# A decode kernel whose loads leave from two queues: every second half of K and V, behind the first ones, is issued from ScalarE's queue, and the order of all work is searched anew

## The chip, the cores and the metric

The kernel runs on one core of a Trainium2 chip. The core has five engines, each with an in-order stream of instructions of its own: TensorE (PE in the profile) for matrix products, VectorE (DVE), ScalarE (ACT), GpSimd (POOL) and SyncE (SP). Sixteen DMA engines move data between HBM and the on-chip memory SBUF; an engine that issues a transfer (here SP, and after the change also ACT) only hands it over, and the transfer then waits in a queue that belongs to the issuing engine. The engines meet through semaphores: an instruction waits until a counter has reached a value.

The metric is device time in microseconds of the whole program. A quoted trace row gives start, duration, engine, source line (L1214 is line 1214 of the kernel), operation and number of instructions.

## What is computed

Two decoder layers, run twice with the same weights, on four tokens (one new position of each of four sequences): attention over a window of a K/V cache, then a gated feed-forward block (FFN). The part that sets the time is the attention:

```python
B, Sq, D = 4, 1, 448
Hq, Hkv, Sk, Dh = 16, 8, 8192, 256
W = min(4096, max(256, Sk // 4))            # 2048 positions
q = (x @ wq).reshape(B, Sq, Hq, Dh).transpose(0, 2, 1, 3)
k = jnp.repeat(k_cache[:, :, Sk - W:, :], rep, axis=1)
v = jnp.repeat(v_cache[:, :, Sk - W:, :], rep, axis=1)
scores = jnp.einsum("bhqd,bhkd->bhqk", q, k) * (Dh ** -0.5)
o = jnp.einsum("bhqk,bhkd->bhqd", _softmax(scores), v)
return o.transpose(0, 2, 1, 3).reshape(B, Sq, Hq * Dh) @ wo
...
x = x + _A_ref(_layernorm(x), A_k_cache, A_v_cache, A_wq, A_wo)
x = x + _B_ref(_layernorm(x), B_w_gate, B_w_up, B_w_down)
x = x + _A_ref(_layernorm(x), A_k_cache, A_v_cache, A_wq, A_wo)
x = x + _B_ref(_layernorm(x), B_w_gate, B_w_up, B_w_down)
```

Each kv head of each token has a K and a V of 2048 x 256 bf16 values, 1 MB each. Both layers read the same cache, and a token's second layer needs the result of its first one, so either its K and V are kept on chip between the two uses or they are loaded twice.

## The kernel before

**Halves and slots.** K and V of a kv head are loaded in halves of 512 KB. In this text K103.1 is half 1 of K of token 1, layer 0, kv head 3 (the program's own order: token, layer, head). A half lies in one of 31 slots of the buffer `kv`; seven more slots (31 to 37) hold the query weights `wq` until the last query projection has read them. The table `SLOTS` gives each load its slot, written here as K103.1@14. A load may be issued only when the last reader of what lay in its slot is done. That reader is the `scores` operation for a half of K (L982) and one `pv` operation for a half of V (L1057). Of the eight heads of a token the last six of its first layer are kept (`KEEP_K`, `KEEP_V`): 6 heads x 4 halves = 24 slots stay occupied until that token's second layer has used them.

**Groups.** Two kv heads of one token make a group. On its way a half of K is turned on VectorE (`tr`, L948). Then follow `scores` (PE, L982), the maximum (DVE, L995), `spread` (PE, L1000), its negative (DVE, L1009), the exponential (ACT, L1013), `turn` (PE, L1026), a copy `pT` (ACT, L1035), `total` (PE, L1043), four `pv` (PE, L1057), a copy `oh` (ACT, L1072), its second step (DVE, L1074), `flip` (PE, L1080) and the scaled result `oT` (DVE, L1090); then the output projection (PE, L1102 and L1110). There are 32 groups, in the order of the table `PLAN`; for every token four of layer 0 and four of layer 1. Of its four layer-1 groups three use the kept heads and load nothing, and the one with heads 0 and 1 loads again.

**Between the layers of a token** stands a serial piece: the rows of the output projection are folded into the residual (L857 on ACT, L859 on DVE, L867 on PE), then the norm (L599 on PE), the FFN (`gu`, 112 matmuls of L785; a tanh on ACT, L805; `down`, 56 matmuls of L826, which needs the weights `wd`), a norm again, the query projection (L671 on PE, L677 on ACT, L687, L701) and the spread queries `qc` (DVE, L706) and `qe` (POOL, L987). Only then can the layer-1 `scores` of that token start and give back the kept slots of K, and the `pv` behind them those of V. This piece, from the landing of the token's last kept half to its first layer-1 `scores`, is called the handover here; there are four, one for each token.

**What sets the order.** Nothing is decided while the program is built. The tables `SEQ_PE`, `SEQ_DVE`, `SEQ_ACT`, `SEQ_POOL` and `SEQ_SP` list, by number, every operation of each engine in the order of its stream (a number counts calls of `g.op` and `g.dma`). They come from a search done ahead. `schedule` (L235) reads them, gives the loads their slots, adds the waits that a reused slot needs, and drops waits that others imply. In `SEQ_SP` a pair "124+126" is one transfer of a whole K into two neighbouring slots. All loads are issued by SP, in order: a load whose slot is not free yet holds up all behind it.

**Fillers.** A "w" in `SEQ_PE` is a matmul that adds zero to the bank `Ab` (L1214). It has no result; it keeps PE occupied. `HELD` says how many fillers each DVE or ACT operation on that bank has to wait for.

Of the kernel before, what the change touches and what calls it, by code (L numbers as in the profile page):

```python
# [38 lines left out]
SLEAD = -3.4  # L39
# [43 lines left out]
).split()  # L83
SEQ_DVE = (
# [18 lines left out]
).split()  # L103
SEQ_ACT = (
# [5 lines left out]
).split()  # L110
SEQ_POOL = (
# [8 lines left out]
).split()  # L120
SEQ_SP = (
# [7 lines left out]
).split()  # L129
# [1161 lines left out]
```

## Time and profile before

| | |
|---|---|
| time, median of 3 runs | 283.76 us (281.19 to 288.03) |
| span of the profiled execution, first to last instruction | 283.0 us |
| busy: PE / DVE / POOL / ACT | 210.4 / 168.6 / 77.2 / 50.9 us |
| moved by the DMA engines | 96.67 MB, mean 342 GB/s |
| issued by SP: halves of V, halves of K, whole K | 80, 66, 7 |
| fillers (L1214) | 147, 51.0 us busy |
| mean clock granted to TensorE | 0.895 |

The profiled execution has no total of its own beside the span; the median of the runs is 0.8 us above it. "Busy" counts an engine's instructions, not its waits, and PE's busy time is modelled at its end, so it doesn't say that PE is at its limit. The DMA engines' rate over time says more here: it is flat near 408 GB/s for long stretches and lower in others.

### The profile page before, as it was taken

What the parts mean: (1) busy time and instruction counts of PE and PEld (TensorE: products, weight loads), DVE (VectorE), ACT (ScalarE), POOL (GpSimd) and SP (SyncE); (2) the same over time, 40 slices, a digit from 0 to 9 for tenths busy, and PEclk for the clock granted to TensorE, in tenths of its full rate; (3) what the DMA queues carried; (4) which work ended last, traced back from release to release, by engine and by line L of the source; (5) the groups of instructions that cost most, each with busy time, mean ns of one, the idle gap of its engine ahead of it and who ended that gap; (6) DMA issues with size and microseconds to landing.
All of it is one profiled execution on the core that took longest, in us unless ns stands there. A gap on an engine that the chain in (4) does not pass through costs nothing.

```text
span 283.0 us, 9526 instructions
## 1 busy us (share of the span) xinstructions
PE 210.4 (74%) x4204; PEld 120.8 (43%) x4204; DVE 168.6 (60%) x511; ACT 50.9 (18%) x123; POOL 77.2 (27%) x202
## 2 busy tenths in 40 slices
PE   0757557586778886789887876798685787888986
PEld 0322124233644543347453432375453346554672
DVE  8745374158226795573755858656756378548831
ACT  0030002011102412112121212112130221034311
POOL 1352103001303432013253241123341221341650
PEclk9997757779789999799997979999795999999995
DMA  6999999999999999968799999948799997899300
GB/s 258 424 414 401 413 410 402 407 401 406 377 390 408 400 408 406 409 278 307 290 324 403 411 406 408 397 170 295 254 316 412 415 405 266 286 341 415 125 2 3
DMA packets 27752, 96.67 MB, mean 342 GB/s; under 512 B 2747, under 2 KB 6847, under 8 KB 26431
## 3 DMA queue, kind: packets, MB, share of 16 engines
q1 hardware_dynamic: 27703, 96.06, 88.0%
q8 instruction: 33, 0.54, 0.8%
q14 instruction: 8, 0.07, 0.1%
q10 hardware_dynamic: 8, 0.00, 0.0%
HBM read 96.05 MB, written 0.00 MB: 339 GB/s over the span
## 4 chain that ended last, share of the span: by engine, by line
DMA 30%; PE 27%; SPq 23%; DVE 12%; issue 3%; ACT 3%; POOL 0%
DMA half<-in_A_k_cache_dram 13%; DMA half<-in_A_v_cache_dram 11%; SPq L555 10%; DVE half L948 8%; SPq L958 8%; DMA wd_sb<-in_B_w_down_dram 6%; PE A L1214 5%; PE Y L1057 5%; PE S L982 4%; PE Z L785 3%; SPq L944 3%; SPq L942 3%; PE Z L826 2%; PE A L1110 2%; DVE oh L1074 1%
## 5 line engine op out<-in xcount | busy, mean ns | idle before, releaser
L948 DVE STREAM_TRANSPOSE half<-half 128x1024 uint32<-128x1024 uint32 x80 | 98.0, 1233 | 16.3 <-DMA half<-in_A_k_cache_dram 15.9
L1214 PE MATMUL A<-identb,small 128*128 128x512 bf16 x147 | 51.0, 452 | 7.4 <-DVE A L478 5.5
L1070 POOL TENSOR_TENSOR small<-small 128x4 f32<-128x4 f32 x32 | 32.4, 1015 | 68.0 <-DVE small L1048 61.7
L982 PE MATMUL S<-half,qe 128*8 128x256 bf16 (+1 forms) x1040 | 40.8, 305 | 12.0 <-DVE half L948 11.1
L1057 PE MATMUL Y<-half,pT 128*8 128x256 bf16 x1024 | 42.2, 296 | 7.3 <-DMA half<-in_A_v_cache_dram 3.9
L982 PEld LDWEIGHTS S<-half,qe 128*8 128x8 bf16 x1040 | 25.4, 92 | 26.1 <-DVE half L948 15.5
L987 POOL TENSOR_TENSOR qe<-qc,tiny 128x64 bf16<-128x64 bf16 x64 | 17.2, 292 | 60.1 <-PE S L982 46.4
L1013 ACT ACTIVATE praw<-S,small 104x256 bf16<-104x256 f32 x32 | 15.1, 473 | 81.7 <-DVE small L1009 81.2
L1057 PEld LDWEIGHTS Y<-half,pT 128*8 128x8 bf16 x1024 | 22.2, 90 | 17.8 <-DMA half<-in_A_v_cache_dram 5.3
L995 DVE TENSOR_REDUCE tiny<-S 104x1 bf16<-104x256 f32 x32 | 13.3, 418 | 19.0 <-PE S L982 19.0
L1072 ACT ACTIVATE oh<-Y 128x256 bf16<-128x256 f32 x32 | 12.3, 383 | 66.3 <-PE Y L1057 61.9
L1214 PEld LDWEIGHTS A<-identb,small 128*128 128x128 bf16 x147 | 13.0, 109 | 20.4 <-issue 7.4
L1074 DVE SCALAR_TENSOR_TENSOR oh<-oh,small,Y 128x256 bf16<-128x256 bf16 x32 | 15.0, 468 | 11.0 <-ACT oh L1072 10.4
L1110 PE MATMUL A<-wo_sb,oT 128*4 128x448 bf16 x220 | 17.2, 380 | 0.8 <-DVE oT L1090 0.6
L1080 PE MATMUL Y<-tiny,oh 128*128 128x4 bf16 x64 | 6.6, 172 | 15.1 <-DVE oh L1074 15.0
L1048 DVE TENSOR_REDUCE small<-Y 128x4 f32<-128x64 f32 x32 | 7.0, 218 | 13.8 <-PE Y L1043 12.1
L1026 PE MATMUL Y<-selt,praw 104*64 104x48 bf16 x256 | 10.1, 197 | 5.9 <-ACT praw L1013 5.5
L1080 PEld LDWEIGHTS Y<-tiny,oh 128*128 128x128 bf16 x64 | 4.2, 103 | 22.5 <-DVE oh L1074 19.6
L1035 ACT ACTIVATE pT<-Y 128x192 bf16<-128x192 f32 x32 | 10.5, 329 | 15.6 <-PE Y L1026 15.3
L1026 PEld LDWEIGHTS Y<-selt,praw 104*64 104x64 bf16 x256 | 6.7, 113 | 12.6 <-ACT praw L1013 9.9
L671 PE MATMUL Z<-half,xn 128*5 128x512 bf16 x160 | 10.2, 379 | 2.2 <-DVE st L606 0.8
L612 POOL TENSOR_SCALAR st<-st 128x1 f32<-128x1 f32 x16 | 4.4, 274 | 26.4 <-DVE st L606 26.4
(125 smaller groups left out, 219.7 us busy)
## 6 DMA issues: line engine op xcount, KB each, us to landing
half<-in_A_v_cache_dram SPq DMA_DIRECT2D x80, 512.0 KB, 12.1
half<-in_A_k_cache_dram SPq DMA_DIRECT2D x66, 512.0 KB, 10.3
half<-in_A_k_cache_dram SPq DMA_DIRECT2D x7, 1024.0 KB, 17.2
wo_sb<-in_A_wo_dram SPq DMA_DIRECT2D x8, 448.0 KB, 16.8
half<-in_A_wq_dram SPq DMA_DIRECT2D x3, 1024.0 KB, 9.0
wd_sb<-in_B_w_down_dram SPq DMA_DIRECT2D x1, 1568.0 KB, 17.1
wg_sb<-in_B_w_gate_dram SPq DMA_DIRECT2D x1, 1344.0 KB, 17.3
wu_sb<-in_B_w_up_dram SPq DMA_DIRECT2D x1, 1344.0 KB, 16.6
```

What stands on the lines that cost most here:

```text
L555: g.dma(rank, nbytes, lambda e: e.dma_start(dst, src), f"w{nw[0]}", w=key if isinstance(key, tuple) else (key,), run=run)
L948: return e.transpose(a, a)
L958: g.dma(pp + VLAG, 1 << 19, lambda e, cell=cell, hv=hv, vsrc=vsrc: e.dma_start(unit(cell), vsrc[hv]), None, w=(f"v{t}_{kvh}_{hv}",), run=4 ...
L982: last = e.matmul(Sb[s_][qd:qd + 8, c0:c0 + rhs.free_size()], lhsT=qe[q_][:, P, ce, :, :].rearrange("p a n -> p (a n)"), rhs=rhs, start=(c ...
L987: g.op(POOL, 0.25, pos - SLEAD - 1, lambda e, P=P, t=t, kvh=kvh: e.tensor_tensor(qe[q_][:, P, :, :, :], qc[t][:, kvh, :, :].unsqueeze(2).b ...
L1013: return e.activation(praw[0:R, 0:128 * n].rearrange("p (g r l) -> p g r l", g=2 * n, l=2), Sb[s_][0:R, 0:128 * n].rearrange("p (l g r) -> ...
L1026: last = e.matmul(Yb[p_][64 * h:64 * h + 64, c0:c0 + (48 if n == 2 else 32)], lhsT=praw[0:R, 64 * gg:64 * gg + 64], rhs=w, start=(gg == 0) ...
L1057: last = e.matmul(Yb[p_][32 * gg:32 * gg + M, 256:512], lhsT=pT[pt][:, gg, 2 * a + hv, 4 * P:4 * P + M] if n == 2 else p1[:, gg % 2, 2 * a ...
L1070: g.op(POOL, 0.69, pos, lambda e: e.tensor_tensor(ri[p_][:, 0:2 * n], rs[p_][:, 0:2 * n], expo[:, 1:1 + 2 * n], op=ALU.pow), r=(f"rs{p_}", ...
L1074: g.op(DVE, 0.43, pos, lambda e: e.scalar_tensor_tensor(out=oh[:, :], in0=oh[:, :], scalar=lomask[:, 0:1], in1=Yb[p_][:, 256:512], op0=ALU ...
L1110: last = e.matmul(Ab[32 * k:32 * k + B, 0:D], lhsT=oT[oi][:, k % 2, k // 2, :], rhs=wo_sb[:, 4 * kvh + k, :], start=False, stop=False, ski ...
L1214: return e.matmul(Ab[:, 0:512], lhsT=zero[:, 0:1].broadcast_to([128, 128]), rhs=identb[:, :].unsqueeze(1).broadcast_to([128, 4, 128]), sta ...
```

## The change

The order of the groups is the same, and so are the slots' number, the heads kept, the bytes moved and what every operation computes. What differs:

1. **Two issuing queues.** 64 of the 153 transfers of K and V, all behind the first ones, carry an "a" in `SEQ_SP`. `schedule` moves them to ScalarE: the transfer stands at its place in `SEQ_ACT`, among the exponentials and copies, with its wait for the slot.
2. **Steps.** `PLAN` had 28 steps, four of them with two groups; it has 32 of one group each. A step ends with its output projection. The form of a group with one head and its constants (`sel1`, `far1`, seven small DVE operations at the start) are taken out; no group had that form. A "/" in `PLAN` would split `scores` in two operations; no group uses it.
3. **All tables are new**: the five orders, `SLOTS`, `HELD`. `SEQ_PE` has 31 fillers, not 147. `SLOTS` leaves no pair of K halves over 15 slots apart (before, K111 was, which took 16 matmuls more).

What the numbers in the tables stand for, in the places that matter (A: is ACT's queue):

```
first loads, before: X WQ2 K000 WQ1 V001.0 WQ3 WQ0 K001.1 K001.0 V000.1 K003 WO0 V000.0 WO5 K004 ...
first loads, after:  K103.0@0 X K004 K005 K100.0@5 K007 K002 K101.0@10 K001.0 K006 K101.1@14 K001.1 WQ3 WQ2 WQ1 WQ0
                     K100.1@16 K003 V000.1 K000 V002.1 WO1 V001.1@23 V003.1 V004.1 WO0 V001.0@26 V002.0 V000.0 WO4 V004.0
                     WO5 A:V005.0 wgb WO2 WO7 WO3 wub V003.0 V007.1 V006.1 A:V007.0 A:V005.1 V006.0 wga WO6 V100.0@26
                     wua wd A:V100.1@23 V101.0@5 K103.1@14 A:V101.1@10 A:K105.1@16 K102.0@26 A:K104.1@23 K107.0@5
                     A:K104.0@10 K105.0@8 A:K102.1@17 ...
handover of token 1, from its last kept half:
  before: V106.0 | K200.0 K201.0 K201.1 V201.0 V200.1 V200.0 V201.1 K010.0 K010.1 K011.1 K011.0 V010.0 V010.1
          V011.1 K203.1 K203.0 V011.0 V203.0 | K205.0
  after:  A:V107.0 | A:K011.0 K011.1 A:V200.0 V200.1 A:V201.0 V201.1 V011.0 A:V010.0 V010.1 A:K202.1 A:V011.1 K203.0
          A:K207.1 K205.0 K204.1 A:K203.1 A:K202.0 | K205.1
handover of token 2:
  before: V206.0 | K301.0 K300.0 K301.1 V300.1 V301.0 V301.1 V300.0 K304.1 K305.1 K302.0 K304.0 K303.1 K303.0
          K302.1 | V306.1
  after:  V207.1 | A:K306.1 V300.0 A:K302.1 V301.0 V301.1 A:K306.0 A:K302.0 V300.1 A:K303.1 K305.1 A:K305.0 | K304.1
handover of token 3:
  before: V307.1 | K111.0 K110.1 K110.0 K210.0 V110.1 K210.1 V110.0 V111.0 K211.0 K211.1 V211.1 V111.1 V210.0 | V210.1
  after:  A:V307.1 | K111.1 A:V111.1 V110.1 A:K210.1 V110.0 A:V111.0 K211.0 A:K210.0 K211.1 A:V210.1 K310.1
          A:K310.0 | V210.0
ACT, after, token 0: ... d.rowsA d.tanh A:K104.1 d.q0 d.q1 oh A:K104.0 A:K102.1 A:K106.0 A:V105.1 exp pT A:K201.1 A:V105.0 exp ...
```

The first bar stands behind the token's last kept half, the second ahead of the first load whose slot waits for that token's layer 1 (for token 3: for its query projection).

The core of the diff, with the long tables cut:

```diff
@@ schedule @@
         seq = {PE: SEQ_PE, DVE: SEQ_DVE, SCA: SEQ_ACT, POOL: SEQ_POOL, SP: SEQ_SP}
-        pairs = [[self.ops[int(y)] for y in x.split("+")] for x in SEQ_SP if "+" in x]
-        order = {e: [self.ops[int(y)] for x in s if x[0] not in "wq" for y in x.split("+")] for e, s in seq.items()}
+        pairs = [[self.ops[int(y)] for y in x.strip("a").split("+")] for x in SEQ_SP if "+" in x]
+        order = {e: [self.ops[int(y)] for x in s if x[0] not in "wq" for y in x.strip("a").split("+")] for e, s in seq.items()}
+        loads = [o for o in order[SP] if o.cell is not None]
+        for x in SEQ_SP:
+            if x[0] == "a":
+                for y in x.strip("a").split("+"):
+                    self.ops[int(y)].eng = SCA
+        order[SP] = [o for o in order[SP] if o.eng == SP]
         assert sum(map(len, order.values())) == len(self.ops) == len({o for s in order.values() for o in s})
-        loads = [o for o in order[SP] if o.cell is not None]
...
-        order[SP] = [o for o in order[SP] if o not in second]
+        for e in (SP, SCA):
+            order[e] = [o for o in order[e] if o not in second]
@@ group @@
-            def scores(e):
+            def scores(e, Ps):
                 last = None
-                X, J = 4 // n, 2 * n
                 for ce in range(8):
-                    for x in range(X):
-                        for P in range(n):
+                    for x in range(2):
+                        for P in Ps:
...
-            o = g.op(PE, (0.87, 1.72)[n - 1], pos - SLEAD, scores, ...
+            for Ps in ([(P,) for P in range(len(members))] if apart[gi] else [tuple(range(len(members)))]):
+                kw = dict(acc=(f"s{s_}",)) if Ps[0] else dict(w=(f"s{s_}",))
+                o = g.op(PE, (0.86, 1.72)[len(Ps) - 1], pos - SLEAD, lambda e, Ps=Ps: scores(e, Ps), ...
...
@@ tables @@
 PLAN = (
-    "000+001", "002+003 004+005", "006+007", "100+101", "012+013", ...
-    "212+213 214+215", "216+217 302+303", "306+305", "304+307", "110+111", "210+211 316+313", "314+315",
+    "000+001", "002+003", "004+005", "006+007", "100+101", "012+013", ...
+    "212+213", "214+215", "216+217", "302+303", "306+305", "304+307", "110+111", "210+211", "316+313", "314+315",
...
+    "128 165 196 150 127 158 121 224 195 225 a201 111 187 262 188 113 164 239 233 a238 a202 232 110 261 322 112 114 "
+    "a323 328 434 a329 a469 426 a463 502 a461 467 a428 582 a496 504 a472 498 588 584 a590 a471 a621 430 a431 465 a436 "
...
 HELD = (
-    "0 44 48 57 72 76 86 96 96 100 100 109 112 122 131 131 133 133 138 138 139 139 139 139 139 139 139 139 141 141"
+    "0 4 4 4 8 8 8 10 10 12 12 12 12 15 29 29 29 29 30 30 30 30 30 30 30 30 30 30 30 30"
```

More of the change, by code (lines that the diff above doesn't have):

```diff
@@ L357, in plan @@
 def plan():
-    return [() if st == "F" else tuple(tuple((int(c[0]), int(c[1]), int(c[2])) for c in b.split("+")) for b in st.split()) for st in PLAN]
+    return [() if st == "F" else tuple(tuple((int(c[0]), int(c[1]), int(c[2])) for c in b.replace("/", "+").split("+")) for b in st.split()) for st in PLAN]
 def build(nc, A_x, A_k_cache, A_v_cache, A_wq, A_wo, B_x, B_w_gate, B_w_up, B_w_down, out):
@@ L401, in build @@
         selt = [at(f"selt{h}", [128, 4, 12], BF16) for h in range(2)]
-        sel1 = [sb(f"sel1{h}", [128, 4, 2, 2, 2], BF16) for h in range(2)]
         small = sb("small", [128, 17 + 2 * NS + 8 * NY + 2 * B], FP32)
@@ L408, in build @@
         fars = small[:, 11:14].bitcast(BF16)
-        far, far1 = fars[:, 0:4].rearrange("p (P o n) -> p P o n", P=2, o=1), fars[:, 4:6].rearrange("p (o n) -> p o n", o=1)
+        far = fars[:, 0:4].rearrange("p (P o n) -> p P o n", P=2, o=1)
         nmask = rs[0]
@@ L436, in build @@
         rest = plan()
+        apart = ["/" in b for st in PLAN for b in st.split()]
         ends = {t: max(i for i, s in enumerate(rest) for b in s for h in b if h[:2] == (t, 1)) for t in range(B)}
@@ L513, in build @@
                 op0=ALU.add, op1=ALU.mult), r=("rs0", "negm0"), w=("far",))
-        for n_ in range(2):
-            g.op(DVE, 0.1, R0, lambda e, n_=n_: e.tensor_tensor(
-                negm[1][:, n_:n_ + 1], nmask[:, n_:n_ + 1], nmask[:, 2 + n_:3 + n_], op=ALU.add), r=("rs0",), w=("negm1",))
-        g.op(DVE, 0.1, R0, lambda e: e.tensor_scalar(
-            far1[:, 0, :], negm[1][:, 0:2], negm[0][:, 1:2], FAR, op0=ALU.add,
-            op1=ALU.mult), r=("negm0", "negm1"), w=("far1",))
-        for h in range(2):
-            for y in range(2):
-                g.op(DVE, 0.16, R0, lambda e, h=h, y=y: e.tensor_copy(sel1[h][:, :, :, y, :], ivq[:, :, h:4:2, :]),
-                     r=("identb",), w=(f"sel1{h}{y}",))
         for s_ in range(NS):
@@ L930, in group @@
             p_, s_, q_ = gi % NY, gi % NS, gi % NQ
-            pt, pos, n = gi % NP, members[-1][0], len(members)
-            R, N, lag = (104, 256, 0.0) if n == 2 else (104, 128, 0.0)
+            pt, pos, n, R, N = gi % NP, members[-1][0], 2, 104, 256
             kcs, kks, vss, free_k, free_v = [], [], [], [], []
@@ L972, in group @@
             g.tag = ("g",) + members[-1][1:]
-            def scores(e):
+            def scores(e, Ps):
                 last = None
-                X, J = 4 // n, 2 * n
                 for ce in range(8):
-                    for x in range(X):
-                        for P in range(n):
+                    for x in range(2):
+                        for P in Ps:
                             qd = 64 * P + 32 * x
-                            for i, (c0, rhs) in enumerate(keys(kcs[P], J * x, J, ce)):
+                            for i, (c0, rhs) in enumerate(keys(kcs[P], 4 * x, 4, ce)):
                                 last = e.matmul(Sb[s_][qd:qd + 8, c0:c0 + rhs.free_size()],
@@ L990, in group @@
                     r=(f"qc{t}_{kvh}",) + tuple(f"qmask{a}" for a in range(4)), w=(f"qe{q_}_{P}",))
-            o = g.op(PE, (0.87, 1.72)[n - 1], pos - SLEAD, scores, r=tuple(k for kk in kks for k in kk) + tuple(f"qe{q_}_{P}" for P in range(n)),
-                     w=(f"s{s_}",), bank=(f"S{s_}",))
-            o.rel = tuple(c for kc, fr in zip(kcs, free_k) if fr for c in kc)
-            o.pairs = tuple(kcs)
+            for Ps in ([(P,) for P in range(len(members))] if apart[gi] else [tuple(range(len(members)))]):
+                kw = dict(acc=(f"s{s_}",)) if Ps[0] else dict(w=(f"s{s_}",))
+                o = g.op(PE, (0.86, 1.72)[len(Ps) - 1], pos - SLEAD, lambda e, Ps=Ps: scores(e, Ps),
+                         r=tuple(k for P in Ps for k in kks[P]) + tuple(f"qe{q_}_{P}" for P in Ps), bank=(f"S{s_}",), **kw)
+                o.rel = tuple(c for P in Ps if free_k[P] for c in kcs[P])
+                o.pairs = tuple(kcs[P] for P in Ps)
             g.op(DVE, (0.23, 0.36)[n - 1], pos, lambda e: e.tensor_reduce(
@@ L1000, in spread @@
                 e.matmul(Sb[s_][0:R, 256:288], lhsT=identb[0:R, 0:R],
-                         rhs=far[0:R, :, :, :].broadcast_to([R, 2, 8, 2]) if n == 2 else
-                         far1[0:R, :, :].broadcast_to([R, 16, 2]), start=True, stop=False, skip_group_check=True)
+                         rhs=far[0:R, :, :, :].broadcast_to([R, 2, 8, 2]), start=True, stop=False, skip_group_check=True)
                 return e.matmul(
@@ L1007, in spread @@
                     skip_group_check=True)
-            g.op(PE, 0.18, pos, spread, r=(f"pmax{s_}", "identb", "far", "far1"), w=(f"m{s_}",), bank=(f"S{s_}",))
+            g.op(PE, 0.18, pos, spread, r=(f"pmax{s_}", "identb", "far"), w=(f"m{s_}",), bank=(f"S{s_}",))
             g.op(DVE, 0.13, pos, lambda e: e.tensor_reduce(
@@ L1021, in turn @@
                     for h in range(2):
-                        if n == 2:
-                            c0, w = 48 * gg, selt[h][0:R, :, :].rearrange("p a u -> p (a u)")
-                        else:
-                            c0, w = 32 * gg, sel1[h][0:R, :, :, :, :].rearrange("p x a y n -> p (x a y n)")
-                        last = e.matmul(Yb[p_][64 * h:64 * h + 64, c0:c0 + (48 if n == 2 else 32)],
-                                        lhsT=praw[0:R, 64 * gg:64 * gg + 64], rhs=w,
+                        last = e.matmul(Yb[p_][64 * h:64 * h + 64, 48 * gg:48 * gg + 48],
+                                        lhsT=praw[0:R, 64 * gg:64 * gg + 64],
+                                        rhs=selt[h][0:R, :, :].rearrange("p a u -> p (a u)"),
                                         start=(gg == 0), stop=False, skip_group_check=True)
                 return last
-            g.op(PE, (0.12, 0.22)[n - 1], pos, turn, r=("praw", "selt0", "selt1") +
-                 tuple(f"sel1{h}{y}" for h in range(2) for y in range(2)), w=(f"yp{p_}",), bank=(f"Y{p_}",))
-            PW = 192 if n == 2 else 64
-            pf = pT[pt][:, :, :, :].rearrange("p g a u -> p (g a u)")[:, 0:PW]
-            p1 = pf[:, 0:64].rearrange("p (c x a y n) -> p c x a y n", c=2, x=4, a=2, y=2)
-            g.op(SCA, (0.2, 0.27)[n - 1], pos, lambda e: e.activation(pf, Yb[p_][:, 0:PW], ACT.Copy),
+            g.op(PE, (0.12, 0.22)[n - 1], pos, turn, r=("praw", "selt0", "selt1"), w=(f"yp{p_}",), bank=(f"Y{p_}",))
+            pf = pT[pt][:, :, :, :].rearrange("p g a u -> p (g a u)")
+            g.op(SCA, (0.2, 0.27)[n - 1], pos, lambda e: e.activation(pf, Yb[p_][:, 0:192], ACT.Copy),
                 r=(f"yp{p_}",), w=(f"pT{pt}",), bank=(f"Y{p_}",))
@@ L1042, in total @@
                 for P in range(n):
-                    last = e.matmul(sums[:, :, P, :], lhsT=onesb[:, 0:1].broadcast_to([128, 128]), rhs=pw[:, :, 8 * P:8 * P + 2] if n == 2 else
-                                    p1[:, :, :, :, 0, :].rearrange("p c x a n -> p (c x a) n"),
+                    last = e.matmul(sums[:, :, P, :], lhsT=onesb[:, 0:1].broadcast_to([128, 128]), rhs=pw[:, :, 8 * P:8 * P + 2],
                                     start=False, stop=False, skip_group_check=True)
@@ L1053, in pv @@
                 last = None
-                M = 4 if n == 1 else 8
                 for a in range(2):
                     for gg in range(4):
-                        last = e.matmul(Yb[p_][32 * gg:32 * gg + M, 256:512],
-                                        lhsT=pT[pt][:, gg, 2 * a + hv, 4 * P:4 * P + M] if n == 2 else
-                                        p1[:, gg % 2, 2 * a + gg // 2, hv, :, :].rearrange("p y n -> p (y n)"),
+                        last = e.matmul(Yb[p_][32 * gg:32 * gg + 8, 256:512],
+                                        lhsT=pT[pt][:, gg, 2 * a + hv, 4 * P:4 * P + 8],
                                         rhs=unit(vss[P][hv])[:, 1024 * a + 256 * gg:1024 * a + 256 * gg + 256], start=False,
```

128 rows, old and new, of tables (PLAN, SEQ_ACT, SEQ_DVE, SEQ_PE) are left out of this document.

## The prediction

> **What bounds the kernel now.** I read the page from the top: the busy shares, the row of GB/s over time, the chain that ended last.
>
> ```profile
> span 283.0 us, 9526 instructions
> ...
> PE 210.4 (74%) x4204; PEld 120.8 (43%) x4204; DVE 168.6 (60%) x511; ACT 50.9 (18%) x123; POOL 77.2 (27%) x202
> ...
> DMA half<-in_A_k_cache_dram 13%; DMA half<-in_A_v_cache_dram 11%; SPq L555 10%; DVE half L948 8%; SPq L958 8%; DMA wd_sb<-in_B_w_down_dram 6%; PE A L1214 5%; PE Y L1057 5%; PE S L982 4%; PE Z L785 3%; SPq L944 3%; SPq L942 3%; PE Z L826 2%; PE A L1110 2%; DVE oh L1074 1%
> ```
>
> No engine is full. The chain changes hands between transfers, SP's queue and short compute pieces. So I asked when the DMA isn't full, with the stretches cut where the GB/s row changes (last column GB/s):
>
> ```profile
> 100.00:120.00 20.00, 14.06 (x249) 6.65 (x245) 13.42 (x29) 3.77 (x9) 3.95 (x11) 0.91 1.03 408
> 120.00:148.00 28.00, 24.08 (x576) 15.71 (x576) 16.36 (x48) 5.41 (x13) 8.62 (x25) 1.00 0.80 299
> 184.00:212.00 28.00, 23.69 (x576) 15.90 (x574) 18.06 (x52) 5.66 (x14) 9.42 (x27) 0.94 0.76 257
> 233.00:256.00 23.00, 19.44 (x505) 13.29 (x507) 14.45 (x49) 4.89 (x11) 7.19 (x21) 1.00 0.87 306
> 256.00:283.00 27.00, 22.36 (x531) 14.30 (x519) 15.12 (x65) 6.64 (x19) 9.48 (x21) 0.85 0.31 124
> ```
>
> Full rate is 408 GB/s, so a half (0.524 MB) takes 1.285 us. Against that rate the three low stretches lose 28 x 109/408 = 7.5, 28 x 151/408 = 10.4 and 23 x 102/408 = 5.8 us, together 23.6 us. The last stretch is the tail behind the last load, which the change hardly touches. The three losses are the handovers of tokens 1, 2 and 3, and SP's own instructions show why: each pair below is the last issue ahead of SP's long silence and the first one behind it.
>
> ```profile
> 111.45 0.84 SPq L958 DMA_DIRECT2D half<-in_A_v_cache_dram  x1
> 126.95 0.33 SPq L958 DMA_DIRECT2D half<-in_A_v_cache_dram  x1
> 170.65 1.01 SPq L958 DMA_DIRECT2D half<-in_A_v_cache_dram  x1
> 187.24 0.33 SPq L958 DMA_DIRECT2D half<-in_A_v_cache_dram  x1
> 222.25 0.77 SPq L942 DMA_DIRECT2D half<-in_A_k_cache_dram  x1
> 237.36 0.33 SPq L958 DMA_DIRECT2D half<-in_A_v_cache_dram  x1
> ```
>
> SP waits 14.7, 15.6 and 14.3 us because no slot is free: 24 of 31 hold a token's kept halves, and the seven left are 7 x 1.285 = 9 us of work for the DMA. **The bound is the bytes at 408 GB/s plus what each handover costs once seven slots are used up.**
>
> **The change part by part.**
>
> *The three handovers.* Slots and kept heads are the same, so the DMA still has only what seven slots turn over. I count it in the decoded load orders: between a token's last kept half and the first load that needs its next layer stand 18, 14 and 13 halves before, 17, 11 and 12 after. Five fewer in all: 5 x 1.285 = 6.4 us more loss, if the handovers last as long. One becomes shorter, since the new order ends each token with halves of V:
>
> ```profile
> 177.72 1.06 PE S L982 x29
> ...
> 179.81 0.48 ACT praw L1013
> ...
> 181.62 1.07 PE Y L1057 x32
> ...
> 188.12 2.82 PE Z L785 x112
> ```
>
> These are pieces of the chain. At token 2 the last group's `scores` and softmax, 177.72 to 181.62, stood behind the landed halves; done ahead, they take 3.9 us out. I take 6.4 - 3.9 = +2.5 us, between -23.6 (all loss gone) and +6.4.
>
> *The first handover*, which costs no bandwidth today:
>
> ```profile
> 64.22 17.12 DMA wd_sb<-in_B_w_down_dram
> 81.39 1.56 PE Z L826 x56
> ...
> 65.34 10.27 SPq L958 DMA_DIRECT2D half<-in_A_v_cache_dram  x1
> 91.04 0.33 SPq L958 DMA_DIRECT2D half<-in_A_v_cache_dram  x1
> ```
>
> `down` starts when `wd` lands, and 9.65 us later the first slot comes free by layer-1 `scores`. Before, 36 halves go ahead of `wd`; after, 38, and three more (V100.1, V101.1, K105.1) leave from ACT while `wd` waits in SP's queue. If the two queues share the engines evenly, the three overtake it: five halves, 6.4 us, so `wd` lands near 88. That is only moved, not lost. But behind `wd` there are then six halves (V101.0, K103.1, K102.0, K104.1, K107.0, K104.0) until layer-1 `scores` frees slot 8: 7.7 us of work. The gap to fill is 9.65 us and the landing of the next load, at least 3.2 us by the rows below: 12.85 - 7.7 = **+5.1 us**, between 0 and 9.0 (the three overtakers' 3.9 us on top).
>
> *The 64 issues on ACT.*
>
> ```profile
> L958 SPq DMA_DIRECT2D half<-in_A_v_cache_dram x80: 327/633/10267, 2.5 to 253.9; - x80
> DMA to landing us min/median/max: 3.2/12.1/18.9
> 248.11 0.43 SPq L942 DMA_DIRECT2D half<-in_A_k_cache_dram  x1
> ACT praw L1013 <- DVE small L1009: 81.2, 25, 7.0
> ```
>
> With room in the queue an issue takes SP 0.33 us (126.95) to 0.43; ACT has none to show, so SP's is the nearest row. 64 x 0.43 = 27.5 us on an engine that is busy for 50.9. ACT waits 81.2 us for the softmax maxima alone, and an issue that stands in such a wait is free. Where several stand in a row it isn't: four stand ahead of the first layer-1 exponential of token 0, three ahead of one of tokens 1 and 2. Beyond the first of each that is 3 + 2 + 2 = 7 issues, 3.0 us; half of it on the path gives **+1.5 us**, between 0 and 27.5. Each also waits for its slot with the exponentials queued behind it, and behind those `turn` and `pv`, which free further slots. The four at token 0 wait for `pv` and `scores` that PE runs ahead of that exponential's maximum, so I add nothing; if that cover is gone, this term grows.
>
> [...]
>
> *116 fillers fewer.* They stand on the chain with 5% (14.2 us), and they keep the clock up (third column from the end):
>
> ```profile
> L1214 PE MATMUL A<-identb,small 128*128 128x512 bf16 x147 | 51.0, 452 | 7.4 <-DVE A L478 5.5
> 212.00:216.00 4.00, 0.39 (x10) 0.31 (x14) 3.30 (x6) 0.43 (x2) 0.23 (x1) 0.71 1.03 418
> 216.00:220.00 4.00, 4.00 (x80) 2.34 (x75) 1.48 (x4) 0.53 (x2) 1.32 (x3) 0.50 1.01 405
> 220.00:224.00 4.00, 2.40 (x63) 1.54 (x65) 2.09 (x7) 0.42 (x2) 1.11 (x3) 0.94 1.03 415
> 116.73 1.70 PE S L982 x30
> 121.39 1.00 PE Y L1057 x32
> 153.25 1.81 PE Y L1057 x32
> ```
>
> Where PE had 0.39 us of work in 4, the clock fell to 0.50 in the next 4, and then came back. A group's `scores` take 1.70 us cold (116.73) and 1.06 warm (177.72), its `pv` 1.81 and 1.00: 1.45 us a group. Without the fillers half of their 14.2 us is gained (behind the other half something else, a norm or a copy, is late anyway): -7.1. One cold group at each of four handovers: +5.8. Net **-1.3 us**, between -14.2 and, if all `scores` and `pv` on the chain (9%, 25 us) ran 1.7 times as long, +17.7.
>
> *The rest.* Sixteen matmuls fewer (no pair of slots far apart any more): 16 x 37 ns by the 29 in 1.06 us at 177.72, -0.6 us. The seven small DVE operations lie under the first loads, the new steps only move output projections: 0; if those were late, they would delay `rows` by one projection, about 0.5 us.
>
> **Sum**: 2.5 + 5.1 + 1.5 - 1.3 - 0.6 = +7.2; 283.0 + 7.2 = 290.2 us of span. The median lies 0.8 above the span: **291.0 us**, 2.6% slower. The runs before reach from 281.19 to 288.03, so 2% is about what can be told from no change.
>
> **The rivals.**
>
> *The stalls halve (faster).* Today one blocked load holds up all behind it, for 15 us at a time; with two queues a load with a free slot can pass. For it: K200, K201, K010 and later K300, K301 now come before the kept halves, so their slots turn early. Against it: my count of halves. If half of 23.6 us goes and the first handover stays full: 283.8 - 11.8 + 1.5 - 1.3 - 0.6 = 271.6 us. It decides from the point where K or V of the next token lands inside SP's old silences.
>
> *No net change.* The first handover finds its loads after all, and shorter handovers balance the five halves: 283.8 + 1.5 - 1.3 - 0.6 = 283.4 us. This is also what comes out if the loads on ACT leave in much the order that SP gave them.
>
> *ACT stands still in issues.* In full stretches SP's issues take nearly as long as a half takes to move (1.01 us at 170.65). If ACT's issues do the same, each costs 1.285, not 0.43; with a third of the 64 on the path, 21 x 0.86 = +18 us: 309 us. For it: the longest issue, 10.27 us, stands behind that of `wd`, where ACT now also issues. Against it: ACT's own queue holds few loads at a time.
> [...]
>
> *A cold PE*: +17.7 instead of -1.3 makes 310 us. Against it: the 120 to 148 stretch has the clock at 1.00 with PE busy mostly with its own work.
>
> **How the numbers follow.** Forecast (290 to 299) 0.32; no net change 0.27; stalls halve 0.25; ACT stands still 0.10; cold PE 0.06. So slower by over 2% 0.48, within 0.27, faster 0.25. The range from 272 to 307 leaves out the lower half of the faster case and most of the last two, under 0.2. The likeliest case's own range is 289.5 to 299.
>
> **What the profile after would show.** Right: `wd` lands near 88 us, and a dip in GB/s follows around 90 to 100 that wasn't there; three further dips worth 20 to 30 us; ACT's issues 0.33 to 0.6 us; the mean clock below that of before. Wrong: dips clearly smaller (then the order found loads that my count of slots misses), ACT issues above 1 us, or exponentials that start late behind them.

## The result and the profile after

The changed kernel takes 291.21 us (median of 4 runs, 288.81 to 292.36) against 284.2 us of the kernel before in the runs beside it: a ratio of 1.027, 95% interval 1.021 to 1.034. It is slower, and 291.0 was forecast. Executions of one kernel lie up to 4% apart here and a profile is one of them, so below a time is a median, and a span only explains. The ratios leave out runs more than 1.5% above the fastest of their kernel, so they are not the quotients of the medians, and some rest on few runs (that of "all loads on SP" on two of ten).

The first lines of its page show the busy engines and the two queues (packets, MB, share of 16 engines' span).

```profile
span 290.2 us, 9246 instructions
...
PE 194.2 (67%) x4072; PEld 115.0 (40%) x4072; DVE 165.5 (57%) x504; ACT 50.1 (17%) x123; POOL 75.9 (26%) x202
...
q1 hardware_dynamic: 18487, 62.50, 55.3%
q10 hardware_dynamic: 9224, 33.56, 30.0%
...
L1202 PE MATMUL A<-identb,small 128*128 128x512 bf16 x31 | 12.5, 424 | 0.0
```

A third of the bytes now goes through ACT's queue (q10). The fillers (last row) went from 51.0 to 12.5 us, 38.5 less, but PE's busy time only from 210.4 to 194.2, 16.2 less: the rest of PE's work takes 22 us more, with 16 matmuls fewer in it. So the question is again when the DMA isn't full. Here are the stretches of the changed kernel, cut where its GB/s change (the third number from the end is the granted clock, the last the GB/s):

```profile
80.00:104.00 24.00, 18.42 (x360) 10.69 (x360) 11.69 (x30) 2.51 (x5) 5.89 (x18) 0.64 0.81 282
132.00:160.00 28.00, 21.67 (x508) 13.95 (x504) 13.35 (x44) 4.84 (x12) 7.10 (x22) 0.86 0.83 308
192.00:212.00 20.00, 14.90 (x383) 10.45 (x379) 10.32 (x32) 2.73 (x6) 7.59 (x24) 0.90 0.66 233
236.00:264.00 28.00, 23.70 (x541) 14.19 (x542) 15.70 (x52) 5.61 (x13) 7.51 (x20) 0.88 0.69 259
```

and two stretches of the kernel before that the prediction did not quote:

```profile
76.00:104.00 28.00, 22.89 (x517) 13.82 (x517) 16.42 (x47) 5.48 (x13) 8.67 (x25) 0.92 1.04 397
124.00:148.00 24.00, 21.09 (x527) 14.18 (x524) 13.82 (x45) 4.69 (x11) 7.61 (x24) 1.00 0.76 280
```

Against 408 GB/s a stretch loses its length times the missing share, 24 x 126/408 = 7.4 us for the first row.

| loss in us at the handover of token | 0 | 1 | 2 | 3 | sum |
|---|---|---|---|---|---|
| before | 0.8 | 7.5 | 10.4 | 5.8 | 24.5 |
| after | 7.4 | 6.9 | 8.6 | 10.2 | 33.1 |

The loss grew by 8.6 us and the span by 7.2 (the tail behind the last load is a little shorter). The time went where the loads stop, above all into the handovers of tokens 0 and 3. The chain and PE's timeline show the first:

```profile
66.51 20.79 DMA wd_sb<-in_B_w_down_dram
87.35 1.61 PE Z L824 x56
...
98.54 0.33 SPq L939
```

`wd` lands at 87.30 (81.34 before), `down` starts, and SP's first load behind it leaves 11.2 us later (9.65 before). What is longer in these 11.2 us is mostly PE's own work. After:

```profile
90.83 3.58 PE L669 MATMUL Z<-half,xn 128*5 128x512 bf16 x32
...
97.38 2.94 PE L978 MATMUL S<-half,qe 128*8 128x256 bf16 x64 [1.27 <-POOL qe L983]
```

Before, the same two pieces, with fillers standing around them:

```profile
84.47 0.82 PE L671 MATMUL Z<-half,xn 128*5 128x512 bf16 x12
...
85.66 1.25 PE L671 MATMUL Z<-half,xn 128*5 128x512 bf16 x20 [0.26 <-DVE xn L589]
...
89.89 1.12 PE L982 MATMUL S<-half,qe 128*8 128x256 bf16 x32
```

The q projection took 2.44 us from start to end (0.82 and 1.25 with a gap between) and takes 3.58, 1.1 us more; the difference to explain is 1.5. The first 32 matmuls of `scores`, which free the slot, take about as long as before (1.12 us; the load leaves 1.16 us after their start). All 64 take 2.94, so it is the second 32, behind that load, that run slowly. PE is cold there: the clock of the stretch is 0.64 against 0.92.

At token 3 the second half of the hole looks the same. These are the two halves of the changed kernel's hole, four windows of the second half (249.02 to 252.43 is the time just ahead of the fall of the clock), and PE's longest wait ahead of that fall:

```profile
236.00:248.00 12.00, 10.33 (x279) 7.02 (x279) 6.64 (x25) 2.45 (x6) 3.74 (x9) 1.00 0.58 226
248.00:264.00 16.00, 13.38 (x268) 7.17 (x265) 9.06 (x28) 3.16 (x7) 3.77 (x12) 0.79 0.77 284
248.00:252.00 4.00, 2.40 (x70) 1.55 (x67) 0.61 (x5) 0.66 (x2) 1.29 (x3) 1.00 0.91 346
249.02:252.43 3.41, 1.86 (x67) 1.61 (x67) 1.00 (x4) 0.38 (x1) 0.27 (x2) 1.00 0.86 303
252.00:256.00 4.00, 3.43 (x52) 1.67 (x52) 3.47 (x12) 0.00 (x0) 0.17 (x1) 0.55 0.97 344
256.00:260.00 4.00, 4.00 (x59) 1.59 (x55) 1.69 (x5) 1.26 (x2) 1.19 (x4) 0.59 0.31 86
```

```profile
250.57 0.71 PE L1046 MATMUL Y<-half,pT 128*8 128x256 bf16 x19 [1.56 <-issue]
```

The first half loses 12 x 182/408 = 5.4 us with the clock at 1.00, about what the whole hole lost before (5.8); the second half loses 16 x 124/408 = 4.9 us more. There, after one lull, the clock is at 0.55 to 0.59 for 8 us in which PE is busy for 7.4, and the loads run dry at 86 GB/s. The kernel before had 1.00 from 233 to 256, by the prediction's row. No wait of PE in 243 to 252 is longer than 1.56 us, and in the 3.41 us ahead of the fall PE was busy for 1.86; what makes the clock fall there is not shown.

### The profile page after: what moved, and what is told of

Read it like the earlier page. It is cut to its first block, busy times and chain, and to the rows that moved or that the text cites. A ratio compares the mean times of both kernels' runs of the same rounds, so it can differ in the third digit from the quotient of the medians.

```text
span 290.2 us, 9246 instructions
## 1 busy us (share of the span) xinstructions
PE 194.2 (67%) x4072; PEld 115.0 (40%) x4072; DVE 165.5 (57%) x504; ACT 50.1 (17%) x123; POOL 75.9 (26%) x202
## 4 chain that ended last, share of the span: by engine, by line
DMA 39%; PE 32%; DVE 15%; SPq 5%; ACT 4%; issue 2%; POOL 1%; ACTq 0%; DVEq 0%
DMA half<-in_A_v_cache_dram 17%; DVE half L945 9%; DMA half<-in_A_k_cache_dram 8%; PE S L978 8%; DMA half<-in_A_wq_dram 8%; PE Y L1046 7%; DMA wd_sb<-in_B_w_down_dram 7%; PE Z L669 4%; PE A L1098 3%; SPq L553 2%; PE Z L824 2%; PE Z L783 2%; DVE oh L1062 1%; ACT wide L675 1%; SPq L939 1%
## 5 line engine op out<-in xcount | busy, mean ns | idle before, releaser
L945 DVE STREAM_TRANSPOSE half<-half 128x1024 uint32<-128x1024 uint32 x80 | 96.8, 1228 | 11.3 <-DMA half<-in_A_k_cache_dram 11.0
L1046 PE MATMUL Y<-half,pT 128*8 128x256 bf16 x1024 | 49.8, 302 | 17.0 <-DMA half<-in_A_v_cache_dram 7.7
L978 PE MATMUL S<-half,qe 128*8 128x256 bf16 x1024 | 44.9, 333 | 13.6 <-DVE half L945 9.1
L1046 PEld LDWEIGHTS Y<-half,pT 128*8 128x8 bf16 x1024 | 20.3, 89 | 28.5 <-DMA half<-in_A_v_cache_dram 9.0
L1010 ACT ACTIVATE praw<-S,small 104x256 bf16<-104x256 f32 x32 | 15.2, 474 | 75.5 <-DVE small L1006 62.8
L1098 PE MATMUL A<-wo_sb,oT 128*4 128x448 bf16 x220 | 21.1, 397 | 3.9 <-DVE oT L1078 3.9
L1062 DVE SCALAR_TENSOR_TENSOR oh<-oh,small,Y 128x256 bf16<-128x256 bf16 x32 | 15.1, 472 | 10.4 <-ACT oh L1060 10.2
L1060 ACT ACTIVATE oh<-Y 128x256 bf16<-128x256 f32 x32 | 12.3, 383 | 36.6 <-PE Y L1046 25.6
L669 PE MATMUL Z<-half,xn 128*5 128x512 bf16 x160 | 15.0, 520 | 4.6 <-DMA half<-in_A_wq_dram 4.6
L1078 DVE TENSOR_TENSOR oT<-Y,small 128x4 bf16<-128x4 f32 x64 | 8.9, 159 | 11.8 <-PE Y L1068 7.6
L584 PE MATMUL Z<-xn,twice 128*128 128x1 bf16 x16 | 2.9, 183 | 16.9 <-DVE xn L602 10.8
L597 PE MATMUL Z<-st,small 128*128 128x2 f32 x32 | 7.7, 311 | 7.3 <-DVE xn L587 3.7
L1202 PE MATMUL A<-identb,small 128*128 128x512 bf16 x31 | 12.5, 424 | 0.0
## 6 DMA issues: line engine op xcount, KB each, us to landing
half<-in_A_k_cache_dram SPq DMA_DIRECT2D x7, 1024.0 KB, 14.2
```

Source lines behind the costliest of these rows:

```text
L669: last = e.matmul(zb[32 * j:32 * j + B + 1, 0:512], lhsT=lhsT, rhs=wq_sb[:, c:c + 512], start=(cc == 0), stop=(cc == 3), skip_group_check= ...
L945: return e.transpose(a, a)
L978: last = e.matmul(Sb[s_][qd:qd + 8, c0:c0 + rhs.free_size()], lhsT=qe[q_][:, P, ce, :, :].rearrange("p a n -> p (a n)"), rhs=rhs, start=(c ...
L1010: return e.activation(praw[0:R, 0:128 * n].rearrange("p (g r l) -> p g r l", g=2 * n, l=2), Sb[s_][0:R, 0:128 * n].rearrange("p (l g r) -> ...
L1046: last = e.matmul(Yb[p_][32 * gg:32 * gg + 8, 256:512], lhsT=pT[pt][:, gg, 2 * a + hv, 4 * P:4 * P + 8], rhs=unit(vss[P][hv])[:, 1024 * a ...
L1062: g.op(DVE, 0.43, pos, lambda e: e.scalar_tensor_tensor(out=oh[:, :], in0=oh[:, :], scalar=lomask[:, 0:1], in1=Yb[p_][:, 256:512], op0=ALU ...
```

## The experiments

The theory by then: two causes, **wd overtaken** (three halves from ACT pass it) and **cold PE** (116 fillers fewer), and little else. The rival is the prediction's own list, with slots and issues at +2.5 and +1.5 and fillers at -1.3. A filler multiplies zeros into a bank, so its number leaves the computation as it is.

| kernel | us, median | ratio to before, 95% interval |
|---|---|---|
| changed kernel | 291.21 | 1.027 [1.021, 1.034] |
| its 31 fillers out | 291.86 | 1.027 [1.015, 1.040] |
| 140 fillers | 288.06 | 1.015 [1.007, 1.023] |
| wd first | 286.74, again 288.01 | 1.021 [1.013, 1.029] (the second) |
| all loads on SP | 288.65 | 1.005 [0.992, 1.019] |
| all on SP, 138 fillers | 287.26 | 1.017 [1.008, 1.026] |
| wd first, 142 fillers | 288.36 | none |
| wd first, 158 fillers | 288.46 | 1.011 [1.001, 1.022] |
| ACT's issue time doubled | 291.76 | 1.037 [1.030, 1.044] |
| longer handovers | 293.60 | 1.033 [1.018, 1.048] |
| before, no fillers | 294.99 | 1.036 [1.023, 1.050] |
| before, half its loads on ACT | 297.23 | 1.043 [1.033, 1.053] |

**wd first.** `wu`'s last part and `wd` leave ahead of V100.0, and the halves that overtook them stand behind `wd` in SP's queue.

```diff
 SEQ_SP, by names
-A:V005.1 V006.0 wga WO6 V100.0 wua wd A:V100.1 V101.0 K103.1 A:V101.1 A:K105.1
+A:V005.1 V006.0 wga WO6 wua wd V100.0 V100.1 V101.0 K103.1 V101.1 K105.1
```

> The kernel after, with wua and wd ahead of V100.0, and V100.1, V101.1 and K105.1 issued by SP behind wd instead of by ScalarE; slots and all else as they were. Theory (at token 0 wd comes five halves later than before, and too little stands behind it): wd lands near 82 us, the dip between 88 and 104 us (6.6 us against full rate) falls below 2 us, and the time falls by about 5 us, to 286 us. Rival (the dip comes from the slots alone, whatever the order of wd): the dip only moves, and the time stays within 1.5 us of 291.

> The changed kernel with the loads of wua and wd ahead of the first halves of token 1's V, a second time, so that its ratio has an interval. Theory first handover (+5.1 us in the prediction): 285 to 288 us, a ratio near 1.01. If the overtaken wd costs nothing: 291 us, 1.027.

`down` in the timeline of the second run, and its first stretch:

```profile
84.84 1.62 PE L824 MATMUL Z<-wide,wd_sb 128*128 128x32 bf16 x56
```

```profile
76.00:100.00 24.00, 17.32 (x402) 11.49 (x402) 12.48 (x38) 2.63 (x7) 5.97 (x19) 0.77 0.94 344
```

`wd` lands at 82.2 us (issued at 62.8, landed 19.4 us later), 5.1 us earlier. The edit puts four halves behind it, the three overtakers and V100.0, and 4 x 1.285 = 5.1. `down` starts 2.5 us earlier and no longer waits for a load; the first loss is 24 x 64/408 = 3.8 us instead of 7.4, and the median is 3.2 to 4.5 us lower. By the ratios it is 0.6%, with intervals that overlap, so the loss and the start of `down` are the surer evidence. Half of the loss stays, at a clock of 0.77.

**Fillers out of both kernels.** The `w` marks leave the PE tables, and `HELD` is all zero.

> The kernel after without its 31 fillers, which leaves out work that has no result. Theory (31 are too few to hold the clock and too few to delay much): within 2 us of 291, the mean clock a little below 0.823. Rival (a cold TensorE is what costs): 3 us or more slower.

> The kernel before without its 147 fillers, the largest of the change's parts taken alone. Theory (half of their 14.2 us on the chain is gained, cold groups at four handovers take 5.8 us back): 1.3 us faster, about 283 us, with the mean clock near that of after, 0.82. Rival 1 (the fillers were plain cost on the chain): up to 14 us faster, 270 us. Rival 2 (the clock is what they buy, and the chain needs it): 5 to 17 us slower, 289 to 301 us; this alone would then explain the whole loss of after.

The changed kernel doesn't change; the kernel before loses 10 us, 6.4 in its profiled span (289.4). Its stretch behind token 1's last kept half:

```profile
124.00:160.00 36.00, 28.29 (x598) 18.09 (x586) 17.46 (x53) 6.29 (x16) 9.41 (x26) 0.62 0.70 257
```

The clock there falls from 1.00 to 0.62 and the loss grows from 7.5 to 13.3 us. The 147 fillers that stand on the chain with 14.2 us bring in more than they cost.

**Fillers back.** 140 of them in the changed kernel's PE table, where its own plan has PE waiting.

> The changed kernel with 140 fillers in PE's waits in place of 31 (the same filler matmul; nothing else differs). Theory clock: the kernel before without its 147 fillers became about 10 us slower, the changed kernel without its 31 the same; so the changed kernel lost about what its fillers were worth, and with 140 it comes back to 281 to 285 us with a mean granted clock of 0.88 or more. Theory bytes (the prediction's): the loss is the first handover and the slots used up, which no filler touches; 289 to 293 us, at whatever clock.

PE's timeline behind `wd`, and the first stretch:

```profile
87.35 1.56 PE L827 MATMUL Z<-wide,wd_sb 128*128 128x32 bf16 x56 [1.14 <-DMA wd_sb<-in_B_w_down_dram]
...
90.54 1.90 PE L672 MATMUL Z<-half,xn 128*5 128x512 bf16 x32
...
95.48 1.07 PE L981 MATMUL S<-half,qe 128*8 128x256 bf16 x32 [0.52 <-POOL qe L986]
```

```profile
80.00:100.00 20.00, 15.90 (x332) 9.58 (x332) 9.69 (x29) 2.39 (x5) 5.86 (x18) 0.88 0.85 292
```

`wd` lands at the same time as in the changed kernel, but the q projection takes 1.90 us instead of 3.58 and `scores` begin at 95.48 instead of 97.38. The loss there is 20 x 116/408 = 5.7 us. The median falls by 3.2 us: less than the clock theory's 6 to 10, more than the rival's nothing. The mean clock came back to 0.857 only.

**Both together**, and 16 more fillers at token 3, where the 142 had left PE cold:

> The changed kernel with the loads of wua and wd ahead of the first three halves of token 1's V (these three and K105.1's place behind wd, from SP) and with 142 fillers. Theory clock: both gains add, 4.5 us for wd and 6 to 10 us for the fillers: 276 to 281 us. Theory bytes: only that of wd, 285 to 288 us.

> The changed kernel with wua and wd ahead of the first halves of token 1's V and 158 fillers: the 142 of the run before and 16 more from 220 us on, around token 3's handover, where that run's clock still fell to 0.50 for 8 us. Theory clock: with the clock at 1.00 there, each cold piece comes 1.5 us sooner, together 2 to 4 us off 285 to 288: 282 to 285 us, within 1% of the kernel before. Theory that only the order of the loads counts there: no change to the 142 fillers, 285 to 288 us.

288.4 and 288.5 us: by the medians the two gains don't add. By the ratios they nearly do: 0.6% and 1.2% alone, 1.6% together with 158 fillers, and the two profiled spans (281.9 and 283.7) look like that too. With these intervals the runs don't decide it. The 16 more bring nothing that can be told: the clock theory of that run missed, and the other had "no change" right but its range wrong by 0.5 us. No version here beats the kernel before.

**All loads on SP**, in the order of the table (the "a" marks go), without and with fillers:

> The kernel after, with all its loads issued by SP again, in the order of the load table; the 64 transfers leave ScalarE's stream and nothing else differs. Theory (the handovers and the three loads that overtake wd at token 0 make the loss; an issue on ScalarE is nearly free): wd lands about 4 us earlier, near 83.5 us, the first dip shrinks by up to 4 us, the later ones stay: about 287 us. Rival 1 (the issues in ScalarE's stream are the cost): back near 284 us, with ScalarE's copies and exponentials earlier everywhere. Rival 2 (the second queue helps, since a load with a free slot passes a blocked one): slower than after, 295 us or more, with longer silences of SP.

> The changed kernel's plan and tables with all loads from SyncE and 138 fillers: both suspected losses undone. Loads on SyncE alone gave 288.7 us, fillers alone 288.1. Theory sum: 2.5 for the queue and 3.2 for the fillers off 291.2 make 285 to 286 us, within 1% of the kernel before. Theory one cause in two guises: 288 us. Theory tables (few halves between the tokens): 288 us or more.

288.65 us, with an interval from 0.8% gained to 1.9% lost, and 287.26. By the medians the queue is worth 2.5 us here, by the ratios (1.005 against 1.027) some 6. The second version, with the fillers back as well, shows no such gain over fillers alone: 287.26 against 288.06, 1.017 against 1.015. The theory that both add (285 to 286) missed. So did the one about `wd` in the first version:

```profile
66.63 19.64 DMA wd_sb<-in_B_w_down_dram
```

With the three overtakers behind it in one queue, `wd` lands at 86.27 us, only 1.0 earlier and not near 83.5 (85.58 in the second version, 1.7 earlier). The first loss of the first version is 32 x 84/408 = 6.6 us (76 to 108, at 324 GB/s). The loads as a whole are a little behind: 390 and 391 GB/s up to 65 us, 395 in the changed kernel, which is 0.8 and 0.6 us. The other 2 us of the expected 3.9 are not explained by these runs.

**The kernel before with half its later loads on ACT**: 62 "a" marks, each issue put into ACT's table at its old time; plan and fillers stay.

> The kernel before, with every second load behind wd (62 of them) issued from ScalarE instead of SyncE, in the same order of slots; plan, tables and fillers stay. It is the change's queue part alone. The prediction's price for the issues is +1.5 us, bounds 0 and 27.5: 284 to 287 us. Theory two queues help (a load with a free slot passes one that waits): 272 to 281 us. Theory ACT stands still: 295 us or more.

12.5 us slower: far beyond the price of the issues, and as far as the theory that ACT stands still had it. The four stretches, two places of the chain that ended last, and SP's issue at the time of ACT's first one there:

```profile
76.00:100.00 24.00, 15.74 (x331) 9.72 (x331) 8.73 (x29) 2.54 (x6) 5.42 (x17) 0.80 0.86 295
128.00:152.00 24.00, 19.45 (x438) 11.93 (x431) 13.27 (x40) 3.92 (x9) 5.62 (x18) 0.93 0.66 252
188.00:216.00 28.00, 20.51 (x471) 13.38 (x467) 17.78 (x48) 4.01 (x10) 7.36 (x22) 0.94 0.59 216
244.00:268.00 24.00, 18.06 (x415) 11.79 (x417) 12.82 (x42) 4.08 (x9) 5.80 (x15) 0.90 0.74 275
```

```profile
65.73 19.59 DMA wd_sb<-in_B_w_down_dram
...
262.25 1.89 ACTq L968
264.18 0.49 ACTq L968
264.70 0.50 ACTq L968
265.25 0.48 ACT praw L1023
```

```profile
262.24 1.89 SPq L952 DMA_DIRECT2D half<-in_A_k_cache_dram  x1
```

`wd` lands 4.0 us later than before (85.32 against 81.34): three halves have passed it, and 3 x 1.285 = 3.9. All four losses grow, together from 24.5 to 36.8 us, 5.9 of the 12.3 at token 0. The span of this execution (299.1) grew by 16.1; the rest is the tail, 21.4 us from the landing of the last half to the end against 17.2. At 262.25 three issues stand in a row on the chain, ahead of the first exponential of a new layer, and take 2.9 us. Of the 62 issues most take 0.33 to 0.4 us, the longest 2.32. That it is mostly the order of the loads and of the work behind them that costs is argued from this, not shown: at tokens 1 to 3 no load was traced to its loss. With its tables searched anew, the changed kernel pays less for its 64.

**ACT's issue time doubled** in the changed kernel:

```diff
             ins = o.emit(eng)
+            if eng_name == SCA and o.cell is not None and o.start > 60:
+                self.extra(eng)    # two copies of 32x1
```

> Behind each load that ScalarE issues after the first exponentials (some 60) stand two small copies on ScalarE, some 0.4 us together, so the ScalarE time of an issue is about doubled. The prediction's +1.5 us (7 issues in a row, half on the path): 292.5 to 293 us. If issues lie on the path one by one: up to 25 us more, 300 us or above. If ScalarE always has room: 291 us.

The group of the copies:

```profile
L412 ACT ACTIVATE spare<-identb 32x1 bf16<-32x1 bf16 x122 | 24.7, 203 | 59.3 <-PE S L989 16.7 <-PE Y L1057 16.6 <-PE Y L1079 7.5
```

24.7 us more on ACT, and 0.5 us more in the median; the spans are 290.0 and 290.2. By the ratios it could be 1%, with intervals that overlap. Both are far from 25 us one by one: ACT has room for nearly all of its issues.

**Longer handovers**: the version without fillers, and 12 of them in a row behind the q projection of tokens 0, 1 and 2.

> The changed kernel without its 31 fillers, and with 12 filler matmuls in a row ahead of the first scores of the next layer, at the handovers of tokens 0, 1 and 2: each becomes 4 to 5 us longer on PE. Theory slots used up (each us of a handover beyond the slots' 9 us of work is a us of time): 291.9 + 12 to 14 = 304 to 306 us, and each dip 4 us deeper. Theory the loads catch up behind it: 293 us or less. The longer wait for K and V also lets the clock stay up; if the clock was the price, less than 291.

The first `scores` at token 0 without the row, and with it:

```profile
97.39 3.50 PE L978 MATMUL S<-half,qe 128*8 128x256 bf16 x64 [1.27 <-POOL qe L983]
```

```profile
96.19 4.26 PE L1202 MATMUL A<-identb,small 128*128 128x512 bf16 x12
100.38 2.04 PE L978 MATMUL S<-half,qe 128*8 128x256 bf16 x64
```

12 fillers take 4.26 us, but the `scores` behind them 2.04 us instead of 3.50, so they end only 1.5 us later. Their clock is 0.52 without the row (97.4 to 100.9) and 1.00 with it (100.4 to 102.4). The expected 12 to 14 us came down to 1.7, no difference that can be told from the version without the row. The loss at token 0 grew from 8.2 to 10.4 us; at tokens 1 and 2 (7.1 and 11.8 without, 6.6 and 11.5 with) it didn't, though PE was late there too. So the test came out weaker than planned, and what there is of it speaks against "each us of a handover is a us" at tokens 1 and 2.

## Why the prediction was right

The total came out to 0.2 us, and the place with it: the loads stop at four handovers instead of three. Of its terms the mechanism of one held in the main, and the others were off in directions that cancel, so that a hit to 0.2 us is luck; the runs scatter by more.

- **First handover, +5.1.** Right in mechanism. `wd` was to land near 88 and landed at 87.30; loads stopped behind it; wd first takes half of the loss back. The size is +6.6. Two numbers of the sum were too small: "9.65 us later the first slot comes free" was carried over from a warm PE, and is 11.2 in the changed kernel; and the load that leaves then (98.54) lands 4.4 us later, not 3.2. How much of the lateness of `wd` the overtakers make is less sure: the three delay it by 4.0 us in the kernel before with loads on ACT, but putting them behind it on SP brought only 1.0 and 1.7.
- **Three handovers, +2.5.** The losses make +2.0 (25.7 against 23.7), but not by the count of halves. By tokens the prediction had +1.3, 0 and +1.3; measured are -0.6, -1.8 and +4.4. Token 3's 4.4 lie beside the cold windows at 252 to 260; the part of its hole with a warm PE lost no more than the whole did before. That seven slots set the price is not shown, and the longer handovers speak against it. The right sum is partly luck.
- **64 issues on ACT, +1.5.** The size can't be told from nothing: twice the time cost 0.5 us in the median. What was missed is that an issue lies beside ACT's other work, as the rows of the last section show. The rival in which ACT stands still in issues falls for the changed kernel: they took 0.33 to 1.17 us, half of them under 0.37. The warning that exponentials queue behind an issue was sound: it shows in the kernel before with loads on ACT, and in one place on the chain of the changed one, where an issue (228.31, 0.64 us) stands straight ahead of an exponential (228.99).
- **116 fillers fewer, -1.3.** This is the step that failed, and its sign with it. "Without the fillers half of their 14.2 us is gained": nothing of this is seen; taking the last 31 out gains nothing either. The cold side came closer: 1.5 us was set for a cold piece, and the q projection alone takes 1.1 us longer from start to end. But it was not counted as one, and the pieces lie in the handovers, where the DMA waits for them. Restoring fillers brings 3.2 us, and in the kernel before they are worth 6 to 10, inside the bound of 17.7 that the rival "a cold PE" took.
- **The rest, -0.6**, is too small to be seen.

The sum as the medians leave it: some 3.2 for the order of `wd` and 3.2 for the clock, each undone alone, most of the 7; by the ratios it is 0.6% and 1.2% of the 2.7%, and the intervals of these versions and of the changed kernel overlap. It stays open whether the two add. If they don't, as the medians say (288.4 and not 291.2 - 6.4 = 284.8), some 1% stays with the plan and its tables, or the two share a place, since an earlier `wd` and a warmer PE end the same wait. No run here tells these apart.

## What to carry to other kernels

A load that everything waits for (here `wd`) must not only be issued early; look also at what another queue issues while it is still in its own, as each such transfer can delay it by its own full time (three halves, 4.0 us, in the kernel before with loads on ACT). Before counting cheap fillers as a gain when they go, read the clock of the windows behind them, and look for pieces on the chain that would run cold while transfers wait for them. And a right total proves no term: compare the losses stretch by stretch.

## What the runs showed of the hardware

*An issue from ACT can leave in the middle of a long one of SP, and beside ACT's own work.* Issues of both queues in the changed kernel, and ACT's instructions at the same time:

```profile
61.17 3.52 SPq L955 DMA_DIRECT2D half<-in_A_v_cache_dram  x1
62.66 0.33 ACTq L955 DMA_DIRECT2D half<-in_A_v_cache_dram  x1
```

```profile
62.66 0.33 ACT L1026 ACTIVATE pT<-Y 128x192 bf16<-128x192 f32 x1 [2.79 <-PE Y L1019]
```

All issues of V from each queue (min/median/max in ns):

```profile
L955 SPq DMA_DIRECT2D half<-in_A_v_cache_dram x44: 327/404/10216, 18.6 to 260.8; - x44
L955 ACTq DMA_DIRECT2D half<-in_A_v_cache_dram x36: 334/348/1170, 0.7 to 262.1; - x36
```

ACT issues in 0.33 us in the middle of an issue that takes SP 3.52 us, and runs a copy at the same time. This long issue of SP does not hold up ACT's. But where both start together, ACT's can be as slow as SP's: in the kernel before with loads on ACT the two of 262.24 and 262.25 took 1.89 us each and ended within 0.01 us, and in the changed kernel those of 258.63 (SP) and 258.72 (ACT) took 1.20 and 1.12. Whether one waits for the other is not shown.

*Two queues share the engines.* Three overtaking halves delay `wd` by 4.0 us in the kernel before with loads on ACT; they take 3.9 us to move. With both queues in use the rate is 408 GB/s in the changed kernel too (108 to 130 us).

*Some waste pays, or costs little.* The 147 fillers of the kernel before are worth 6 to 10 us. A row of 12 fillers of 4.26 us delays the end of the `scores` behind it by 1.5 us only: they run at a clock of 1.00 instead of 0.52.
